# Which row groups a score group takes: chosen when it is issued, with longer planned GpSimd pieces and new seeds

## The chip, the cores and the metric

The kernel runs on one core of a Trainium2 chip. The metric is the time of one execution on the device in microseconds (us). Before the change three runs gave 784.35, 784.41 and 786.95 us; the median is 784.41 us. The core has five instruction queues that run beside each other: TensorE (PE, matmuls; its weight loads are listed as PEld), VectorE (DVE), ScalarE (ACT), GpSimd (POOL) and SyncE (SP, which issues the DMA transfers).

## What is computed

One transformer block with a conditioning vector, on 2048 tokens of width 512. Attention has 32 heads of width 16, so the 2048 x 2048 scores of 32 heads are the bulk of the element-wise work.

```python
mod = silu(c) @ w_mod                       # six vectors: sa, ca, ga, sb, cb, gb
h = layernorm(x) * (1 + ca) + sa
qkv = h @ wqkv                              # 32 heads of width 16
p = softmax(q @ k.T * 16 ** -0.5)           # per head, 2048 x 2048
x = x + ga * ((p @ v) @ wo)
h = layernorm(x) * (1 + cb) + sb
x = x + gb * (gelu(h @ w1 + b1) @ w2 + b2)  # inner width 1376
```

## The kernel before

**The score work.** Queries come in four blocks of 512, keys in sixteen tiles of 128 (`kt`). The work is cut into 32 runs (`runs`, `NR`, line 789), and a run handles four row groups at once: TensorE is used as four strips of 32 rows (`rows`, line 841), so that four matmuls with 32 rows each can run side by side, one for each strip. A run and a key tile give a tile of four score units, one for each row group; a unit is 128 keys x 512 queries. There are 32 x 16 x 4 = 2048 units.

**Two ways to exponentiate.** A unit goes one of two ways.

- ScalarE takes groups that alternate between three units and two (`SPAN`, line 306). `qk_a` (line 853) issues the matmuls of a group into a PSUM buffer `st` (there is one of each size), and one ScalarE instruction turns the group into `pt` (line 891). The three or two units follow each other through the tiles in the fixed order of row groups 0, 1, 2, 3: a tile's first three units may end one group, and its last one open the next (`at["A"]`, lines 802 and 856 to 864).
- VectorE takes whole tiles. `qk_d` (line 904) issues one matmul at a time into one of the two PSUM buffers `ax`, on any row group that the tile still lacks (the one that is free first, line 206), and VectorE writes the unit as a 16-bit integer into `ph` (line 933), which read as bf16 is a coarse power of two. Four shifted copies of the tile refine it (`shifts`, line 943): each is one VectorE instruction into `sh` (line 954), or, for the last of the four, four GpSimd pieces of one row group each into `sg` (`by_pool`, lines 962 to 975). The five versions are summed by TensorE, with V scaled in five ways (`VX`).

Of a run's sixteen tiles the five in `DKS` (line 302) may go to either engine: `next_tile` (line 821) gives them to VectorE, and ScalarE takes those that are left when its own are used up. So the share of each engine falls out of the order.

**Products, projections, tails.** `pv_op` (line 977) multiplies a tile by V into `od`, four matmuls side by side, accumulated over a run. `normalise` (line 1027) divides by the sums. When a block of queries is done, `block_tail` (line 1207) runs the output projection, the second layer norm (statistics and `z` on VectorE, `rs` on GpSimd, lines 622 to 638), its transposes, the two MLP matmuls, GELU on ScalarE, and the store. The last block is split in halves; `last_half` (line 1278) is what follows the last score.

**What sets the order.** The kernel writes its instruction order itself. `Plan` (line 107) keeps a clock for each engine, with planned durations given to each operation (`Op`), and again and again commits the operation that can start first (`step`, `pick`, `commit`). It is a list planner that runs when the program is built; the chip only sees the resulting queues. Parts of it that the change touches or that the text speaks of:

- `start` (line 135) gives the planned start of an operation. A score matmul group needs its row groups free (`pe_start`, `tiles`); an operation with `port` on VectorE or GpSimd waits until the other engine's planned piece with `port` is over.
- TensorE has three modes: scores (`qk`), products (`pv`) and the full array (`full`); a change costs 0.107 us in the plan (line 130).
- `G_US` (line 308) is the planned length of a GpSimd piece of `by_pool`, 0.65 us. A piece is planned beside a VectorE instruction that leaves room for it (`beside`, line 187).
- `heat` (line 447) puts filler matmuls with zeros where TensorE would otherwise be idle.
- Among operations that can start at about the same time, the one with the smallest priority value wins, to which `spread` (line 159) adds up to 0.15. That amount is a hash of the operation's kind (on TensorE) or of the source line of its function (other engines) with one of 32 numbers in `SEEDS` (line 64), one for each 25 us of planned time. Other seeds, or other line numbers, give another order.

Of the kernel before, what the change touches and what calls it, by code (L numbers as in the profile page):

```python
# [4 lines left out]

# [6 lines left out]
ACT = mybir.ActivationFunctionType  # L12
# [42 lines left out]
PEA = 0.38  # L55
# [4 lines left out]
DPL = 0.08  # L60
AL = 0.055
FILL = 2.1
SPREAD = 0.15
SEEDS = (925, 529, 257, 846, 939, 899, 560, 662, 544, 155, 536, 522, 19, 893, 450, 795, 742, 2, 4, 794, 818, 153, 176, 144, 484, 633, 742, 123, 569, 63, 333, 698)
HEAT = 1.7


class Res:


    def __init__(self, name, n, alloc):
        self.name, self.alloc = name, alloc
        self.free = [0.0] * n


class Op:
    count = 0

    def __init__(self, eng, fn, us, deps=(), lat=0.14, prio=5.0, mode=None, kind="", acq=None,
                 rel=(), gate=None, port=False):  # L80
        self.port = port
        self.eng, self.fn, self.us, self.lat, self.prio = eng, fn, us, lat, prio
        self.mode, self.kind, self.acq, self.rel, self.gate = mode, kind, acq, rel, gate
        self.end = None
        self.ready = 0.0
        self.tile = None
        self.slot = None
        self.kb, self.due, self.extra = 0, 1e9, False
        self.uses, self.use, self.alt = 0, 1.0, False
        self.rows, self.cont, self.run = None, False, None  # L90
        self.waiters = []
        self.todo = 0
        self.seq = Op.count
        Op.count += 1
        for d in deps:
            if d is None:
                continue
            if d.end is None:
                d.waiters.append(self)
                self.todo += 1  # L100
            else:
                self.ready = max(self.ready, d.end)
        for owner in rel:
            owner.uses += 1


class Plan:
    SLACK = {"NIL": 0.0, "PE": 0.10, "DVE": 0.05, "ACT": 0.15, "POOL": 0.05, "SP": 0.05}

    def __init__(self, dyn, later):  # L110
# [6 lines left out]
        self.dve = (0.0, 0.0, True)  # L117
        self.dyn, self.done, self.fill = dyn, deque(), FILL

# [13 lines left out]
        return max([self.free["PE"]] + [self.tiles.get(i, 0.0) for i in op.mode[1:]])  # L133

    def start(self, op):
        s = max(op.ready, self.pe_start(op) if op.eng == "PE" else self.free[op.eng])
        if op.acq is not None:
            s = max(s, min(op.acq.free))
        if op.eng == "PE" and self.later(op):
            s = max(s, self.fill_at)  # L140
        if op.port and op.us > 0:
            s = max(s, self.port["POOL" if op.eng == "DVE" else "DVE"])
        if op.kind == "beside":
            s = max(s, self.dve[0])
        return s

    def pick(self, eng):
# [11 lines left out]
    def spread(self, o):  # L159
        x = ((sum(map(ord, o.kind)) if o.eng == "PE" else o.fn.__code__.co_firstlineno if o.fn else 0) * 2654435761 ^ SEEDS[min(int(self.now // 25.0), len(SEEDS) - 1)] * 2246822519) & 0xFFFFFFFF  # L160
        x = ((x ^ x >> 15) * 2246822519) & 0xFFFFFFFF
        return SPREAD * ((x ^ x >> 13) & 1023) / 1024.0

# [106 lines left out]
def kernel(  # L270
# [14 lines left out]
    nc = tc.nc  # L285
    P = 128
    S = 2048
    D = 512
# [3 lines left out]
    QB = 512  # L292
# [12 lines left out]
    MM = 0.2155  # L305
    SPAN = (3, 2)
    POOL_US, POOL_MIN = 0.68, 0.5
    G_US, G_MIN, G_PRIO, G_MAX, G_FROM, G_TILES = 0.65, 0.5, 1.0, 4, 60.0, 6
    A_US = {1: 0.49, 2: 0.9165, 3: 1.3435}
    AHEAD = 3  # L310
    FIRST_DKS, D_TIME = (14,), 8.0
# [10 lines left out]
    def res(name, n, shape, dt, pool=work):  # L322
        return Res(name, n, lambda i: pool.tile(shape, dt, name=f"{name}{i}"))
# [3 lines left out]
    r_st = [res(f"st{n}", 1, [P, n * QB], FP32, ps) for n in SPAN]  # L327
    r_od = res("od", 1, [P, QB], FP32, pp)
    r_ax = res("ax", 2, [P, QB], FP32, pp)
    r_pt = [res(f"pt{n}_", NPT, [P, n * QB], BF16) for n in SPAN]  # L330
# [23 lines left out]
    units = [0]  # L354
    queued = deque()
# [45 lines left out]
    plan = Plan(dyn, later)  # L401
# [3 lines left out]
    def op(eng, *a, **k):  # L405
        o = Op(eng, *a, **k)
        if eng == "PE":
            o.due = due_now[0]
            due_now[0] += due_now[1]
        return plan.add(o)  # L410
# [108 lines left out]
    for h in range(2):  # L519
        o_x0 += 2 * [dma(lambda o, h=h: nc.sync.dma_start(out=o_x[0].tile[:, 2 * h:2 * h + 2, :],  # L520
                                                         in_=x_src[0][:, 2 * h:2 * h + 2, :]),
# [55 lines left out]
    for b in range(NQ):  # L577
        late = (lambda: True) if b == 0 else (lambda: first_ln[0])
# [9 lines left out]
    def silu(o):  # L588
# [8 lines left out]
              prio=0.0, rel=(o_tr,))  # L597
# [196 lines left out]
    def run_heads(r):  # L794
        b, u = runs[r]
        return (u % NC, None, u // NC) if b == LAST else (u // 2, u % 2, None)
# [2 lines left out]

    shared = [[kt for kt in (DKS if r else FIRST_DKS)] for r in range(NR)]  # L800
    own = [[kt for kt in range(NT) if kt not in shared[r]] for r in range(NR)]
    at = {"A": [0, 0, 3], "D": [0, 0, []]}
    turn = [0]

    o_e = {}
    left = [0] * NR
    begun = [False] * NR
    o_od = [None] * NR
# [2 lines left out]
    a_run = [0]  # L811
    pv_left = {}

    def d_run():
        for r in range(max(at["D"][0], a_run[0]), NR):
            if shared[r] and (r > a_run[0] or D_TIME < sum(queued) + 1.75 * (
                    len(own[r]) + len(shared[r]) - 1)):
                return r
        return NR

    def next_tile(which, r):
        while r < NR:
            if which == "A" and own[r]:
                return r, own[r].pop(0)
            if which == "A" and shared[r]:
                left[r] -= NPH - 1
                return r, shared[r].pop()
            if which == "D" and shared[r] and r >= d_run():
                return r, shared[r].pop(0)
            r += 1  # L830
        return None

    def qk(o, k, r, kt, i):
        b = runs[r][0]
        cc, par, hb = run_heads(r)
        kb, ko = divmod(kt, TPB)
        qm = o_q[(cc, b)][0]
        q_left[(cc, b)] -= 1
        if q_left[(cc, b)] == 0:
            qm.uses -= 1  # L840
        rows = slice(32 * i, 32 * i + 32)
        nc.tensor.matmul(out=o.tile[:, k * QB:(k + 1) * QB],  # L842
                         lhsT=kT[cc][kb][rows, ko * P:(ko + 1) * P],
                         rhs=qm.tile[rows, par, :] if hb is None else
                         qm.tile[rows, :, hb * HB:(hb + 1) * HB], start=True, stop=True)

    def qk_deps(r, kt):
        want_q(r // 2 + 1 if r < LAST * 8 else r - LAST * 4 + 2)
        cc, par, hb = run_heads(r)
        qm, evs = o_q[(cc, runs[r][0])]  # L850
        return [evs[par or 0], o_k[(cc, kt // TPB)]], qm

    def qk_a():
        got = []
        while len(got) < SPAN[turn[0]]:
            r, kt, i = at["A"]
            if i == 3:
                n = next_tile("A", r)
                if n is None:
                    break  # L860
                r, kt = n
            i = (i + 1) % 4
            at["A"][:] = r, kt, i
            got.append((r, kt, i))
        if not got:
            return
        n = turn[0]
        turn[0] = (n + 1) % len(SPAN)
        live["A"] += 1
        deps, rel = [], []  # L870
        for r, kt, i in got:
            d, qm = qk_deps(r, kt)
            deps += d
            if qm not in rel:
                rel.append(qm)

        def go(o):
            n_a[0] += 1
            queued.append(A_US[len(got)])
            a_run[0] = got[-1][0]  # L880
            for k, u in enumerate(got):
                qk(o, k, *u)
            live["A"] -= 1
        o = op("PE", go, MM, deps, lat=PEA, mode=("qk",) + tuple(u[2] for u in got), kind="qkA", acq=r_st[n],
               rel=rel, gate=lambda: n_a[0] - n_a[1] < 2)

        def ex(e):
            n_a[1] += 1
            queued.popleft()
            units[0] += len(got)  # L890
            nc.scalar.activation(out=e.tile[:, 0:len(got) * QB], in_=o.tile[:, 0:len(got) * QB],  # L891
                                 func=ACT.Exp, scale=ESC)
        e = op("ACT", ex, A_US[len(got)], (o,), lat=AL, prio=1.0, acq=r_pt[n], rel=(o,))
        e.uses += len({u[:2] for u in got})
        for k, (r, kt, i) in enumerate(got):
            o_e[(r, kt, i)] = (e, k)
            if i == 3:
                src = [o_e.pop((r, kt, m)) for m in range(4)]
                es = list({id(x): x for x, _ in src}.values())
                pv_op(r, kt, 0, es, lambda src=src: [x.tile[:, m * QB:(m + 1) * QB] for x, m in src], es)  # L900
                for x in es:
                    x.uses -= 1

    def qk_d():
        r, kt, rows = at["D"]
# [465 lines left out]
    for b in range(NQ):  # L1371
        kind = f"in{b}"
# [40 lines left out]

    state = {"late": 0}
    qk_a()
    want_q(1)
    while True:
        if not live["A"]:
            qk_a()
# [5 lines left out]
        while ended:  # L1425
            r = ended.pop(0)
            if r < NR - 1:
                normalise(r)
            b, u = runs[r]
# [77 lines left out]
```

## Time and profile before

| | |
|---|---|
| median of three runs | 784.41 us |
| profiled execution | 785.1 us |
| its span, first to last instruction | 783.2 us |
| mean granted TensorE clock | 0.998 of full |
| ScalarE: exponentials (line 891) | 624 groups, 710.8 us busy |
| VectorE: evacuations (line 933) | 488, 321.9 us |
| VectorE: shifted copies (line 954) | 405, 284.4 us |
| GpSimd: pieces of shifted copies (line 969) | 332, 205.3 us |
| first exponential starts, last ends | 14.54 us, 760.34 us |

A row of the profile's groups reads: line, engine, operation, output <- input with partitions x elements and type, how many; then busy time and the mean of one in ns; then the engine's idle time just before them and what ended most of it. Instructions of an engine can overlap at their ends, so the mean times the count can exceed the busy time. A row of the timeline reads: start, length, engine, line, operation, output <- input, how many were merged; in brackets the idle time ahead of it and what ended that.

### The profile page before, as it was taken

The page shows a single profiled execution, that of the slowest core. Times are in us where ns is not written, and L with a number is a line of the kernel's source. Part 1 is how long each engine was busy: PE and PEld are TensorE (multiplying, and loading weights), DVE is VectorE, ACT ScalarE, POOL GpSimd, SP SyncE. Part 2 cuts the span into 40 slices and gives each one's busy share as a digit, 9 for nine tenths or more (in the row PEclk, how much of TensorE's full clock was granted, in tenths as well). Part 3 has the DMA queues.
Part 4 walks back from the last instruction along what each step waited for, and adds up shares of the span by engine and source line. Part 5 has one row for each costly group of instructions (what it writes and reads, how often), then busy time and mean ns, then how long its engine had stood idle before and what let it go on. Part 6 is the DMA issues. An engine that isn't in the chain of part 4 may idle for free. (4 is left out here: it accounts for less than half of the span.)

```text
span 783.2 us, 21425 instructions
## 1 busy us (share of the span) xinstructions
PE 746.6 (95%) x8547; PEld 270.9 (35%) x8547; DVE 715.4 (91%) x1229; ACT 752.0 (96%) x675; POOL 337.3 (43%) x639
## 2 busy tenths in 40 slices
PE   8999999999999999999999999999999999989998
PEld 3433333233322232232332222222234434434444
DVE  6787778989999999999999998999899999997984
ACT  4999999999999999999999998999999999999994
POOL 6533545444445445552345243444243354343331
PEclk9999999999999999999999999999999999999999
DMA  7143011100110002000101000000111010100100
GB/s 216 37 151 63 19 23 44 26 16 10 46 52 22 5 17 66 20 9 17 46 21 34 23 19 16 20 23 26 29 42 35 8 41 18 46 19 22 25 18 28
DMA packets 38550, 27.75 MB, mean 35 GB/s; under 512 B 17941, under 2 KB 33846, under 8 KB 38450
## 3 DMA queue, kind: packets, MB, share of 16 engines
q1 hardware_dynamic: 38442, 26.39, 12.5%
q8 instruction: 67, 1.10, 0.6%
q14 instruction: 33, 0.27, 0.1%
q10 hardware_dynamic: 8, 0.00, 0.0%
HBM read 20.77 MB, written 2.61 MB: 30 GB/s over the span
## 5 line engine op out<-in xcount | busy, mean ns | idle before, releaser
L891 ACT ACTIVATE pt<-st 128x1536 bf16<-128x1536 f32 x624 | 710.8, 1302 | 8.3 <-PE st L842 5.7
L933 DVE TENSOR_SCALAR ph<-ax 128x512 int16<-128x512 f32 x488 | 321.9, 679 | 25.0 <-PE ax L842 22.0
L969 POOL TENSOR_SCALAR sg<-ph 128x512 int16<-128x512 int16 x332 | 205.3, 627 | 306.1 <-DVE sh L954 201.1
L954 DVE TENSOR_SCALAR sh<-ph 128x2048 int16<-128x2048 int16 x405 | 284.4, 723 | 4.1 <-PE od L1004 2.9
L842 PE MATMUL st<-qm,kT 32*128 32x512 bf16 x1560 | 245.9, 383 | 13.0 <-ACT pt L891 9.6
L842 PE MATMUL ax<-qm,kT 32*128 32x512 bf16 x488 | 170.2, 379 | 3.9 <-DVE ph L933 2.5
L842 PEld LDWEIGHTS <-kT 32*128 32x128 bf16 x2048 | 76.3, 91 | 229.3 <-issue 219.7
L1004 PE MATMUL od<-sh,VX 128*32 128x512 bf16 (+1 forms) x2024 | 145.3, 342 | 5.9 <-DVE sh L954 5.2
L1004 PE MATMUL od<-pt,VEB 128*32 128x512 bf16 (+1 forms) x1948 | 140.4, 340 | 0.1
L1004 PEld LDWEIGHTS <-VX 128*32 128x32 bf16 x2448 | 61.0, 95 | 89.5 <-issue 77.4
L1004 PEld LDWEIGHTS <-VEB 128*32 128x32 bf16 x2560 | 61.4, 96 | 77.2 <-issue 63.6
L1004 PE MATMUL od<-ph,VEB 128*32 128x512 bf16 (+1 forms) x612 | 48.6, 340 | 1.2 <-DVE OD L1029 1.1
L1237 PE MATMUL ax<-blk,W 128*128 128x512 bf16 (+1 forms) x176 | 44.6, 355 | 1.6 <-DVE ph L933 0.9
L776 POOL TENSOR_SCALAR VX<-VEB 128x128 bf16<-128x128 bf16 x80 | 27.6, 346 | 39.6 <-DVE VEB L652 35.0
L1056 POOL TENSOR_TENSOR OT<-OD,RB 128x256 bf16<-128x256 f32 x38 | 28.5, 764 | 28.7 <-DVE sh L954 18.5
L721 PE MATMUL ax<-blk,w 128*128 128x512 bf16 x124 | 35.6, 381 | 1.5 <-DVE ph L933 0.9
L1177 PE MATMUL ax<-w,g 128*128 128x512 bf16 x128 | 34.8, 382 | 1.2 <-DVE ph L933 1.2
L1004 PE MATMUL od<-sg,VX 128*32 128x512 bf16 (+1 forms) x424 | 34.4, 338 | 0.4 <-POOL sg L969 0.3
L467 PE MATMUL od<-warm 128*32 128x512 bf16 x320 | 31.5, 388 | 0.0
L1242 DVE TENSOR_SCALAR g<-ax,b1c 128x512 bf16<-128x512 f32 (+1 forms) x44 | 29.2, 673 | 0.4 <-PE ax L1237 0.3
L1056 POOL TENSOR_TENSOR OS<-OD,RB 128x256 bf16<-128x256 f32 x24 | 17.1, 728 | 18.2 <-DVE sh L954 18.1
L626 DVE BATCH_NORM_STATS2 ln_s<-xb 128x6 f32<-128x512 bf16 x32 | 21.6, 676 | 1.3 <-DMA xb<-in_A_x_dram 1.2
(108 smaller groups left out, 410.6 us busy)
## 6 DMA issues: line engine op xcount, KB each, us to landing
RB<-rn SPq DMA_DIRECT2D x124, 64.0 KB
xb<-in_A_x_dram SPq DMA_DIRECT2D x7, 512.0 KB
out_dram<-o SPq DMA_DIRECT2D x16, 128.0 KB
qm<-qs SPq DMA_DIRECT2D x120, 16.0 KB
W<-in_B_w_dram SPq DMA_DIRECT2D x1, 1376.0 KB
w<-in_A_wqkv_dram SPq DMA_DIRECT2D x3, 384.0 KB
blk<-in_w_mod_dram SPq DMA_DIRECT2D x2, 512.0 KB
g<-in_w_mod_dram SPq DMA_DIRECT2D x2, 512.0 KB
```

Of the source, the lines that this page charges most:

```text
L467: nc.tensor.matmul(out=o_od[r].tile[32 * i:32 * i + 32, :], lhsT=warm[:, 0:32], rhs=warm[:, 0:1].to_broadcast([P, QB]), start=False, stop= ...
L721: return chain([(lambda ps, j=j: nc.tensor.matmul(out=ps[:, 0:QB], lhsT=w.tile[:, j, cc * P:(cc + 1) * P], rhs=o_h[b].tile[:, j, :], start ...
L842: nc.tensor.matmul(out=o.tile[:, k * QB:(k + 1) * QB], lhsT=kT[cc][kb][rows, ko * P:(ko + 1) * P], rhs=qm.tile[rows, par, :] if hb is None ...
L891: nc.scalar.activation(out=e.tile[:, 0:len(got) * QB], in_=o.tile[:, 0:len(got) * QB], func=ACT.Exp, scale=ESC)
L933: nc.vector.tensor_scalar(out=ph.tile[:, o.row * QB:(o.row + 1) * QB], in0=o.tile, scalar1=PH_B, scalar2=0.0, op0=ALU.add, op1=ALU.max)
L954: nc.vector.tensor_scalar(out=o.tile, in0=first.tile, scalar1=PH_SH[j], scalar2=None, op0=ALU.add)
L969: after_dve(nc.gpsimd.tensor_scalar(out=sh.tile[:, c], in0=first.tile[:, c], scalar1=1.0, scalar2=float(PH_SH[j]), op0=ALU.mult, op1=ALU.add))
L1004: nc.tensor.matmul(out=o_od[r].tile[32 * i:32 * i + 32, n * HB:n * HB + w], lhsT=v_tile(kt, ph)[:, c0:c0 + 32], rhs=got[i][:, at:at + w], ...
L1056: two = beside(lambda c: nc.gpsimd.tensor_tensor(out=OT.tile[:, c], in0=OD.tile[:, c], in1=o5.tile[:, c], op=ALU.mult), (OT,), (OD, o5), f ...
L1177: nc.tensor.matmul(out=ps, lhsT=g[:, f, col:col + P], rhs=rhs, start=(f == 0), stop=(f == NF - 1))
L1237: mm = chain([(lambda ps, f=f, j=j, f0=f0: nc.tensor.matmul(out=ps[:, (f - f0) * N:(f - f0 + 1) * N], lhsT=W1[:, j, f * P:(f + 1) * P], rh ...
L1242: ev.append(op("DVE", lambda o, f=f, f0=f0, mm=mm: nc.vector.tensor_scalar(out=g.tile[:, f, 0:N], in0=mm.tile[:, (f - f0) * N:(f - f0 + 1) ...
```

## The change

- A ScalarE group no longer takes row groups in the fixed order. It is created with a number of units from one or two tiles (class `Tile` keeps which row groups a tile still lacks); which ones is chosen by `choose`, called each time its start is computed. `choose` tries the combinations and prefers the one whose row groups are free first; among equals, one that leaves a row group that VectorE's current tile still lacks. The tile's product with V then finds its four units by row group (`src`).
- `HOLD` is a longest time for which a ScalarE score group may be held back for a VectorE unit when TensorE is in another mode; it is 0.0, so that the new loop in `start` moves nothing.
- `G_US`, the planned length of a GpSimd piece, goes from 0.65 to 0.70 us.
- `SEEDS` has 32 other numbers. As lines are added, all later source lines move by 10 to 32, and these are part of the same hash.

No tile, buffer, data type or engine of an operation is changed.

```diff
@@ -1,5 +1,5 @@
 from collections import deque
-from itertools import islice
+from itertools import combinations, islice
 from contextlib import ExitStack
 import math
 
@@ -60,8 +60,9 @@
 DPL = 0.08
 AL = 0.055
 FILL = 2.1
+HOLD = 0.0
 SPREAD = 0.15
-SEEDS = (925, 529, 257, 846, 939, 899, 560, 662, 544, 155, 536, 522, 19, 893, 450, 795, 742, 2, 4, 794, 818, 153, 176, 144, 484, 633, 742, 123, 569, 63, 333, 698)
+SEEDS = (650, 213, 63, 336, 324, 364, 339, 395, 941, 438, 324, 33, 944, 780, 750, 866, 575, 626, 251, 357, 730, 442, 4, 383, 330, 53, 641, 829, 848, 541, 85, 264)
 HEAT = 1.7
 
 
@@ -86,6 +87,7 @@
         self.tile = None
         self.slot = None
         self.kb, self.due, self.extra = 0, 1e9, False
+        self.choose = None
         self.uses, self.use, self.alt = 0, 1.0, False
         self.rows, self.cont, self.run = None, False, None
         self.waiters = []
@@ -133,6 +135,8 @@
         return max([self.free["PE"]] + [self.tiles.get(i, 0.0) for i in op.mode[1:]])
 
     def start(self, op):
+        if op.choose is not None:
+            op.choose()
         s = max(op.ready, self.pe_start(op) if op.eng == "PE" else self.free[op.eng])
         if op.acq is not None:
             s = max(s, min(op.acq.free))
@@ -142,6 +146,12 @@
             s = max(s, self.port["POOL" if op.eng == "DVE" else "DVE"])
         if op.kind == "beside":
             s = max(s, self.dve[0])
+        if op.kind == "qkA" and self.mode != "qk":
+            for d in self.lists["PE"]:
+                if d.kind == "qkD" and d.gate():
+                    t = max(d.ready, min(d.acq.free))
+                    if s < t <= min(s + HOLD, self.need() - op.us - PEA - 0.02):
+                        s = t
         return s
 
     def pick(self, eng):
@@ -305,7 +315,7 @@
     MM = 0.2155
     SPAN = (3, 2)
     POOL_US, POOL_MIN = 0.68, 0.5
-    G_US, G_MIN, G_PRIO, G_MAX, G_FROM, G_TILES = 0.65, 0.5, 1.0, 4, 60.0, 6
+    G_US, G_MIN, G_PRIO, G_MAX, G_FROM, G_TILES = 0.70, 0.5, 1.0, 4, 60.0, 6
     A_US = {1: 0.49, 2: 0.9165, 3: 1.3435}
     AHEAD = 3
     FIRST_DKS, D_TIME = (14,), 8.0
@@ -799,10 +809,9 @@
 
     shared = [[kt for kt in (DKS if r else FIRST_DKS)] for r in range(NR)]
     own = [[kt for kt in range(NT) if kt not in shared[r]] for r in range(NR)]
-    at = {"A": [0, 0, 3], "D": [0, 0, []]}
+    at = {"A": [None, 0], "D": [0, 0, []]}
     turn = [0]
 
-    o_e = {}
     left = [0] * NR
     begun = [False] * NR
     o_od = [None] * NR
@@ -850,56 +859,79 @@
         qm, evs = o_q[(cc, runs[r][0])]
         return [evs[par or 0], o_k[(cc, kt // TPB)]], qm
 
+    class Tile:
+        def __init__(self, r, kt):
+            self.r, self.kt, self.rows, self.src, self.es = r, kt, [0, 1, 2, 3], {}, []
+
     def qk_a():
-        got = []
-        while len(got) < SPAN[turn[0]]:
-            r, kt, i = at["A"]
-            if i == 3:
-                n = next_tile("A", r)
-                if n is None:
+        got, want = [], SPAN[turn[0]]
+        while want:
+            cur, n = at["A"]
+            if n == 0:
+                nxt = next_tile("A", cur.r if cur else 0)
+                if nxt is None:
                     break
-                r, kt = n
-            i = (i + 1) % 4
-            at["A"][:] = r, kt, i
-            got.append((r, kt, i))
+                cur, n = Tile(*nxt), 4
+            c = min(n, want)
+            want -= c
+            at["A"][:] = cur, n - c
+            got.append((cur, c, c == n))
         if not got:
             return
         n = turn[0]
         turn[0] = (n + 1) % len(SPAN)
         live["A"] += 1
         deps, rel = [], []
-        for r, kt, i in got:
-            d, qm = qk_deps(r, kt)
+        for x, _, _ in got:
+            d, qm = qk_deps(x.r, x.kt)
             deps += d
             if qm not in rel:
                 rel.append(qm)
+        total = sum(c for _, c, _ in got)
+
+        def choose():
+            ks = got[0][1]
+            best = None
+            for head in combinations(got[0][0].rows, ks):
+                for tail in combinations([i for i in range(4) if i not in head], got[1][1] if len(got) > 1 else 0):
+                    busy = head + tail
+                    late = max(plan.tiles.get(i, 0.0) for i in busy) if plan.mode == "qk" else 0.0
+                    k = (max(late, plan.now), not any(i not in busy for i in at["D"][2] or range(4)))
+                    if best is None or k < best[0]:
+                        best = k, busy
+            o.mode = ("qk",) + best[1]
 
         def go(o):
             n_a[0] += 1
-            queued.append(A_US[len(got)])
-            a_run[0] = got[-1][0]
-            for k, u in enumerate(got):
-                qk(o, k, *u)
+            queued.append(A_US[total])
+            a_run[0] = got[-1][0].r
+            k = 0
+            for x, c, _ in got:
+                for i in o.mode[1 + k:1 + k + c]:
+                    qk(o, k, x.r, x.kt, i)
+                    x.rows.remove(i)
+                    x.src[i] = (e, k)
+                    k += 1
             live["A"] -= 1
-        o = op("PE", go, MM, deps, lat=PEA, mode=("qk",) + tuple(u[2] for u in got), kind="qkA", acq=r_st[n],
+        o = op("PE", go, MM, deps, lat=PEA, mode=("qk",) + tuple(range(total)), kind="qkA", acq=r_st[n],
                rel=rel, gate=lambda: n_a[0] - n_a[1] < 2)
+        o.choose = choose
 
         def ex(e):
             n_a[1] += 1
             queued.popleft()
-            units[0] += len(got)
-            nc.scalar.activation(out=e.tile[:, 0:len(got) * QB], in_=o.tile[:, 0:len(got) * QB],
+            units[0] += total
+            nc.scalar.activation(out=e.tile[:, 0:total * QB], in_=o.tile[:, 0:total * QB],
                                  func=ACT.Exp, scale=ESC)
-        e = op("ACT", ex, A_US[len(got)], (o,), lat=AL, prio=1.0, acq=r_pt[n], rel=(o,))
-        e.uses += len({u[:2] for u in got})
-        for k, (r, kt, i) in enumerate(got):
-            o_e[(r, kt, i)] = (e, k)
-            if i == 3:
-                src = [o_e.pop((r, kt, m)) for m in range(4)]
-                es = list({id(x): x for x, _ in src}.values())
-                pv_op(r, kt, 0, es, lambda src=src: [x.tile[:, m * QB:(m + 1) * QB] for x, m in src], es)
-                for x in es:
-                    x.uses -= 1
+        e = op("ACT", ex, A_US[total], (o,), lat=AL, prio=1.0, acq=r_pt[n], rel=(o,))
+        e.uses += len(got)
+        for x, _, full in got:
+            x.es.append(e)
+            if full:
+                pv_op(x.r, x.kt, 0, x.es, lambda x=x: [y.tile[:, m * QB:(m + 1) * QB] for y, m in (
+                    x.src[i] for i in range(4))], x.es)
+                for y in x.es:
+                    y.uses -= 1
 
     def qk_d():
         r, kt, rows = at["D"]
```

## The prediction

> **What bounds the kernel now.** First the busy times, then the costliest groups, both on the page.
>
> ```profile
> PE 746.6 (95%) x8547; PEld 270.9 (35%) x8547; DVE 715.4 (91%) x1229; ACT 752.0 (96%) x675; POOL 337.3 (43%) x639
> ...
> L891 ACT ACTIVATE pt<-st 128x1536 bf16<-128x1536 f32 x624 | 710.8, 1302 | 8.3 <-PE st L842 5.7
> L933 DVE TENSOR_SCALAR ph<-ax 128x512 int16<-128x512 f32 x488 | 321.9, 679 | 25.0 <-PE ax L842 22.0
> L969 POOL TENSOR_SCALAR sg<-ph 128x512 int16<-128x512 int16 x332 | 205.3, 627 | 306.1 <-DVE sh L954 201.1
> L954 DVE TENSOR_SCALAR sh<-ph 128x2048 int16<-128x2048 int16 x405 | 284.4, 723 | 4.1 <-PE od L1004 2.9
> ```
>
> Four engines share one job: 2048 score units of 128 x 512. ScalarE exponentiates 1560 of them (L891, groups of three and two units); VectorE makes the other 488 by integer arithmetic (L933, then four shifted copies of each tile of four units, at L954, or in four pieces on GpSimd, L969). ScalarE's 710.8 us hold only 8.3 us of waiting, so it is the pacemaker. Next I read busy time by stretches of 25 us (columns: stretch, length, then PE, weight loads, DVE, ACT, POOL, clock, DMA).
>
> ```profile
> 50.00:75.00 25.00, 24.90 (x243) 8.44 (x240) 21.04 (x40) 25.00 (x23) 5.03 (x15) 1.00 0.45 126
> 75.00:100.00 25.00, 24.10 (x263) 9.13 (x260) 19.08 (x31) 25.00 (x23) 16.01 (x32) 1.00 0.07 15
> 100.00:125.00 25.00, 23.88 (x253) 9.18 (x249) 20.54 (x34) 25.00 (x23) 12.01 (x22) 1.00 0.16 41
> 125.00:150.00 25.00, 24.52 (x281) 7.59 (x278) 22.81 (x43) 25.00 (x23) 11.56 (x18) 1.00 0.07 18
> ...
> 225.00:250.00 25.00, 23.74 (x253) 7.30 (x250) 25.00 (x43) 25.00 (x23) 12.76 (x21) 1.00 0.10 21
> ...
> 475.00:500.00 25.00, 24.19 (x248) 7.61 (x241) 23.92 (x41) 23.79 (x22) 9.58 (x15) 0.97 0.08 24
> ```
>
> Before 150 us VectorE has room, after 175 us nearly none (25.00 of 25 in one stretch). Between 25 and 750 us ScalarE is idle for 7.2 us in all: the gaps are what a better order can still win. The largest stands in the timeline near 473 us.
>
> ```profile
> 470.99 0.73 DVE L637 TENSOR_SCALAR z<-xb,mv,rs 128x512 bf16<-128x512 bf16 x2 [0.90 <-POOL rs L633]
> ...
> 472.38 0.38 PE L699 MATMUL ax<-ident,z 128*128 128x128 bf16 x4 [1.51 <-DVE ph L933]
> ...
> 473.30 1.45 ACT L891 ACTIVATE pt<-st 128x1536 bf16<-128x1536 f32 x1 [0.81 <-PE st L842]
> ...
> 476.21 2.44 ACT L891 ACTIVATE pt<-st 128x1024 bf16<-128x1024 f32 x2 [1.46 <-PE st L842]
> ```
>
> VectorE's z waited for GpSimd's rs; an evacuation behind z held a buffer of TensorE's transposes; TensorE stood 1.51 us with ScalarE's next scores queued behind. Then the clock fell: in five-us stretches it is 0.79 (470 to 475) and 0.87 (475 to 480), that is (0.21 + 0.13) x 5 / 0.5 = 3.4 us at half rate. ScalarE lost 0.81 + 1.46 = 2.27 us, the largest part of the 7.2.
>
> **The change part by part.** It changes no shape; it changes which unit goes to which engine, and the order. I compared the instruction lists of both programs.
>
> *ScalarE.* L891 has 624 groups now and 623 after: 311 of three, 311 of two, one of a single unit; 1556 units, four fewer. A pair (three and two) costs 710.8 / 312 = 2.278 us; 311 pairs cost 708.5. The group of one is in no row: pro rata 0.46 us (710.8 / 1560), from above 0.63 (ScalarE's cast of 128x512, 627 ns). I take 0.6, as the fixed cost of an instruction stays: 709.1, so -1.7 us (-1.8 to -1.6), straight on the pacing engine.
>
> *VectorE and GpSimd.* One key tile more on VectorE: 492 evacuations instead of 488; shifted copies 411 instead of 405, four for the tile and two taken back from GpSimd, whose pieces fall from 332 to 324 (two tiles of four). VectorE pays 4 x 0.660 (321.9 / 488) + 6 x 0.702 (284.4 / 405) = 6.85 us. What hides it: by the 97th ScalarE group the new order has ten more VectorE steps issued (177 against 167), and ten more is also the total at the end (1196 against 1186). That group runs at about 130 us (the 18th starts at 39.6 us, and 79 groups of 1.13 us lead from it to the 97th); in 50 to 150 us VectorE is idle for 3.96 + 5.92 + 4.46 + 2.19 = 16.5 us. So 0. Without that cover it is +6.85 (third rival).
>
> *TensorE.* Four more products with V, at 0.22 us each (two such sets start at 483.99 and 484.21 us): 0.9 us. Changes between score, product and full-array matmuls: 1305 before, 1328 after. One costs 0.10 us: from a product to the next scores it is 0.31 to 0.32 us start to start (484.21 to 484.53) where two products take 0.22. That is 2.3 us, 3.2 with the products. TensorE also has 20 more filler steps (63 to 83), issued only where nothing else can start, 20 x 0.22 = 4.4 us. I read these as room that covers the 3.2 us: 0 (0 to +3.2).
>
> The Trainium skill, TensorEngine Tiling (Array Packing), Key Properties, says that changing the tiling mode drains TensorE, which speaks against an order with more changes. The trace agrees, with 0.10 us each; were none of the 23 covered, the sum would be 2.3 us higher, 783.9 us.
>
> *The row choice itself.* A ScalarE group takes three or two of four row groups; a VectorE unit beside it can run at once only in another. Neighbouring pairs on a common row: ScalarE's first 51 before, 44 after; VectorE's first 42 and 45. Counting for each run of scores how often its most used row is passed, the sum is 729 before and 731 after, for the same 2048 units. The freedom gains nothing countable: 0, at most 4 pairs x 0.2 us = -0.8.
>
> *Longer GpSimd pieces* (0.65 to 0.70 us planned, 627 ns measured) and *new seeds* redraw the order everywhere; the source lines moved too, and they enter the same tie-break. Their price is that of the gaps: from -7.2 us (all gone) up to +4.5 (two more falls of the clock like that of 473 us). I take -1.1: the one known fall is an accident of one order, and I count half of its 2.27 us as gone, since the new lists have the same rs, z and transposes with GpSimd pieces ahead of rs at most of the seven places in the middle.
>
> *The tail.* Now the last exponential ends at 760.34 us, two GpSimd pieces run until 761.60, and the last product starts behind them.
>
> ```profile
> 754.80 5.54 ACT L891 ACTIVATE pt<-st 128x1024 bf16<-128x1024 f32 x5 [0.19 <-PE st L842]
> ...
> 760.39 1.20 POOL L969 TENSOR_SCALAR sg<-ph 128x512 int16<-128x512 int16 x2 [4.00 <-DVE g L1242]
> ...
> 761.64 0.38 PE L1004 MATMUL od<-sg,VX 128*32 128x256 bf16 x5 [0.30 <-POOL sg L969]
> ```
>
> Afterwards the last product hangs on a VectorE copy (0.68 us) behind two evacuations (0.87): no GpSimd piece, but 1.55 us in its place. I take 0, between -1.2 (the pieces' time gone) and +0.7. The rest of the tail has the same instructions. No DMA is added: 469 instructions on SP in both.
>
> *Sum:* -1.7 - 1.1 = -2.8 on the profiled execution's 785.1 us (span 783.2 and 1.9 around it): 782.3. The median of the runs is 0.7 below it (784.41), so **781.6 us**. Own range: 779 to 784.4.
>
> **Rivals.** (1) *The gaps thin out.* Without the fall of the clock and with half of the other 4.9 us, it is 784.4 - 1.7 - 2.3 - 2.5 = 777.9; 775.5 with no gap left. For it: most gaps (0.2 to 0.8 us) are a copy stretched beside GpSimd, with TensorE's next scores behind it, and longer planned pieces aim at these. Against it: those stretches come from all GpSimd work, not only these pieces.
>
> (2) *The change does not do what it says:* rows gain nothing, gaps return elsewhere, TensorE pays part of its 3.2 us: 784.4 - 1.7 + (1.7 to 4.8) = 784.4 to 787.5. For it: 731 against 729.
>
> (3) *Slower: VectorE becomes the bound.* Place: 175 to 700 us, where it is 98% busy. If the early lead is lost there (a z that waits for rs, as at 471 us), each lost us is paid, up to all 6.85 us: 784.4 + 6.85 - 1.7 = 789.6, and 791.3 if ScalarE's saving turns into waiting. It decides once over 5.6 us (3.9 + 1.7) of VectorE work lands on the path. Against it: the ten steps are done by 130 us, and the lead in scores holds later (461 against 456 at group 577).
>
> **Chances.** Forecast 0.45, (1) 0.25, (2) 0.17, (3) 0.13. About 0.5%, 3.9 us, is what a measurement can tell from no change: faster is below 780.5, slower above 788.3. The forecast's case gives 0.15 to faster; with (1) that is 0.40. Slower 0.13, within 0.47. The range leaves out the best half of (1) and all of (3) with the end of (2): 776.5 to 787.5.
>
> **What would show it.** L891 with 623 groups and about 709 us busy; idle before it near 6 us (forecast), under 4 (1), over 10 (2). The mean clock without a fall, or a fall with a stall of over 1 us ahead of it. VectorE about 7 us busier between 50 and 150 us; if it is so only after 175 us, my cover was wrong. The last exponential ends near 757.5 us, and 22.5 to 23 us follow it. The forecast is wrong if ScalarE's idle time moves by more than 3 us either way: its price is the one I could not read from a row.

## The result, and the profile after

The changed kernel takes 780.17 us (median of seven runs, 779.59 to 782.67) against 785.81 us for the kernel before beside it: a ratio of 0.9938, with a 95% interval of 0.9922 to 0.9954, or 4.9 us less (3.6 to 6.1; the ratio goes by the means, the two medians lie 5.6 us apart). A second measurement (e9 below) gave 0.9927 (0.9912 to 0.9943). The prediction was 781.6 us, faster, with a range of 776.5 to 787.5.

The busy times and the costliest groups of the page after (line 924 was 891, 965 was 933, 1001 was 969, 986 was 954):

```profile
PE 746.1 (96%) x8617; PEld 272.7 (35%) x8617; DVE 715.4 (92%) x1239; ACT 748.8 (96%) x674; POOL 331.1 (43%) x631
...
L924 ACT ACTIVATE pt<-st 128x1536 bf16<-128x1536 f32 x623 | 707.7, 1308 | 5.1 <-PE ax L851 2.0
L965 DVE TENSOR_SCALAR ph<-ax 128x512 int16<-128x512 f32 x492 | 323.5, 682 | 24.1 <-PE ax L851 21.3
L1001 POOL TENSOR_SCALAR sg<-ph 128x512 int16<-128x512 int16 x324 | 198.4, 621 | 285.6 <-DVE sh L986 211.7
L986 DVE TENSOR_SCALAR sh<-ph 128x2048 int16<-128x2048 int16 x411 | 278.1, 704 | 1.8 <-PE od L1036 0.9
```

ScalarE's exponentials are busy for 3.1 us less (710.8 to 707.7) and wait 3.2 us less (8.3 to 5.1). VectorE has ten instructions more in these two groups and the same busy time in all, 715.4 us: the copies' mean fell from 723 to 704 ns.

The profiled execution's span is 777.8 us, 5.4 less than before. It is the fastest of the seven, and its clock did not fall in the middle of the run as it does in the profile before; three of the other six had a mean clock of 0.995 or 0.996. Cut at the first and the last exponential it falls into three:

| stretch of the profiled execution | before | after |
|---|---|---|
| up to the first exponential | 14.5 us | 15.1 us |
| first to last exponential | 745.8 us | 739.5 us |
| of it, ScalarE idle | 8.8 us | 5.7 us |
| after the last exponential | 22.9 us | 23.2 us |

So all of the gain lies between the first and the last exponential. The start is no part of it: in other executions of the changed kernel's order the first exponential came at 13.95 and 14.53 us.

Busy time by stretches, after (columns as before; the third number behind the comma is VectorE):

```profile
50.00:75.00 25.00, 24.47 (x253) 8.74 (x252) 21.48 (x41) 25.00 (x24) 6.76 (x18) 1.00 0.44 126
75.00:100.00 25.00, 24.10 (x263) 10.34 (x259) 20.98 (x36) 24.82 (x23) 13.67 (x28) 1.00 0.06 16
100.00:125.00 25.00, 24.04 (x266) 8.23 (x258) 22.39 (x37) 25.00 (x24) 12.01 (x25) 1.00 0.13 36
125.00:150.00 25.00, 24.92 (x282) 7.97 (x278) 23.03 (x44) 24.99 (x24) 13.92 (x22) 1.00 0.09 24
150.00:175.00 25.00, 24.15 (x278) 8.60 (x270) 24.05 (x40) 25.00 (x24) 12.87 (x26) 1.00 0.05 14
```

The fifth stretch before:

```profile
150.00:175.00 25.00, 23.85 (x271) 7.99 (x269) 22.70 (x39) 24.93 (x23) 11.95 (x24) 1.00 0.08 21
```

VectorE's four stretches from 50 to 150 us sum to 87.9 us, against 83.5 before, and the fifth to 24.05 against 22.70. So VectorE did 5.8 us more work where it had been idle, and ScalarE stayed at 24.8 to 25.0 of 25 there.

The end of the score work, in the timeline after:

```profile
737.25 17.33 ACT L924 ACTIVATE pt<-st 128x1024 bf16<-128x1024 f32 x16 [0.26 <-PE st L851]
...
752.42 1.78 POOL L1001 TENSOR_SCALAR sg<-ph 128x512 int16<-128x512 int16 x3 [3.37 <-DVE g L1274]
...
755.52 0.69 DVE L986 TENSOR_SCALAR sh<-ph 128x2048 int16<-128x2048 int16 x1
...
756.25 0.40 PE L1036 MATMUL od<-sh,VX 128*32 128x256 bf16 x8
```

The last exponential ends at 754.58 us. The GpSimd pieces are done by 754.2, and the last product starts at 756.25, behind a copy on VectorE: 1.67 us after the exponential. Before, it was the product behind the GpSimd pieces that came last; its last five matmuls started 1.30 us after the exponential. One lag took the place of the other.

### The profile page after: what moved, and what is told of

Its sections match the earlier page's. It is cut to its first block, busy times and chain, and to the rows that moved or that the text cites. A ratio compares the mean times of both kernels' runs of the same rounds, so it can differ in the third digit from the quotient of the medians.

```text
span 777.8 us, 21575 instructions
## 1 busy us (share of the span) xinstructions
PE 746.1 (96%) x8617; PEld 272.7 (35%) x8617; DVE 715.4 (92%) x1239; ACT 748.8 (96%) x674; POOL 331.1 (43%) x631
## 4 chain that ended last, share of the span: by engine, by line
PE 46%; ACT 27%; DVE 16%; issue 7%; DMA 2%; POOL 1%; SPq 0%; DVEq 0%; POOLq 0%; ACTq 0%
ACT pt L924 25%; PE od L1036 15%; PE st L851 13%; DVE ph L965 6%; DVE sh L986 5%; PE ax L1209 5%; PE ax L851 3%; PE ax L1269 3%; PE ax L731 2%; DMA dc<-dn 2%; PE od L477 1%; PE ax L1203 1%; DVE xb L1252 1%; PE ax L461 1%; PE ax L770 1%
## 5 line engine op out<-in xcount | busy, mean ns | idle before, releaser
L924 ACT ACTIVATE pt<-st 128x1536 bf16<-128x1536 f32 x623 | 707.7, 1308 | 5.1 <-PE ax L851 2.0
L1001 POOL TENSOR_SCALAR sg<-ph 128x512 int16<-128x512 int16 x324 | 198.4, 621 | 285.6 <-DVE sh L986 211.7
L986 DVE TENSOR_SCALAR sh<-ph 128x2048 int16<-128x2048 int16 x411 | 278.1, 704 | 1.8 <-PE od L1036 0.9
L851 PE MATMUL ax<-qm,kT 32*128 32x512 bf16 x492 | 166.4, 379 | 2.0 <-DVE ph L965 1.2
L1036 PE MATMUL od<-sh,VX 128*32 128x512 bf16 (+1 forms) x2048 | 147.3, 342 | 5.3 <-DVE sh L986 4.2
L477 PE MATMUL od<-warm 128*32 128x512 bf16 x368 | 34.8, 382 | 0.0
L1036 PE MATMUL od<-sg,VX 128*32 128x512 bf16 (+1 forms) x416 | 32.8, 337 | 0.6 <-POOL sg L1001 0.5
```

Of the source, the lines that this page charges most:

```text
L477: nc.tensor.matmul(out=o_od[r].tile[32 * i:32 * i + 32, :], lhsT=warm[:, 0:32], rhs=warm[:, 0:1].to_broadcast([P, QB]), start=False, stop= ...
L851: nc.tensor.matmul(out=o.tile[:, k * QB:(k + 1) * QB], lhsT=kT[cc][kb][rows, ko * P:(ko + 1) * P], rhs=qm.tile[rows, par, :] if hb is None ...
L924: nc.scalar.activation(out=e.tile[:, 0:total * QB], in_=o.tile[:, 0:total * QB], func=ACT.Exp, scale=ESC)
L986: nc.vector.tensor_scalar(out=o.tile, in0=first.tile, scalar1=PH_SH[j], scalar2=None, op0=ALU.add)
L1001: after_dve(nc.gpsimd.tensor_scalar(out=sh.tile[:, c], in0=first.tile[:, c], scalar1=1.0, scalar2=float(PH_SH[j]), op0=ALU.mult, op1=ALU.add))
L1036: nc.tensor.matmul(out=o_od[r].tile[32 * i:32 * i + 32, n * HB:n * HB + w], lhsT=v_tile(kt, ph)[:, c0:c0 + 32], rhs=got[i][:, at:at + w], ...
```

## The experiments

Line numbers enter the planner's tie-break, so every variant keeps each line where it was. A variant that edits the plan has another order throughout; one that edits only which row groups are written out keeps the order of every instruction.

**e1: old seeds.** Only the seeds go back.

```diff
-SEEDS = (650, 213, 63, 336, 324, 364, 339, 395, 941, 438, 324, 33, 944, 780, 750, 866, 575, 626, 251, 357, 730, 442, 4, 383, 330, 53, 641, 829, 848, 541, 85, 264)
+SEEDS = (925, 529, 257, 846, 939, 899, 560, 662, 544, 155, 536, 522, 19, 893, 450, 795, 742, 2, 4, 794, 818, 153, 176, 144, 484, 633, 742, 123, 569, 63, 333, 698)
```

> The changed kernel with the 32 seeds of before; row choice and 0.70 us pieces stay. Its instruction list has 1564 units on ScalarE (626 groups) against 1556. Theory (the gain is that of one good order, found by its seeds: fewer ScalarE units and fewer gaps): 8 units x 0.455 us = +3.6 us, and the gaps between 25 and 750 us back to some 7 us from 4.7, so about 786 us, nothing left of the gain. Rival A (the row choice earns the gain): at most 782 us. Rival B (the longer planned pieces earn it): at most 782 us as well.

Measured: 793.94 us, ratio 1.0117 (1.0099 to 1.0136), slower than the kernel before. The theory's sign held (nothing was left of the gain) and its number, 786 us, failed: from the first to the last exponential it took 744.5 us, less than before the change, but 32.0 us followed the last one. The timeline there:

```profile
762.45 1.58 PE L1269 MATMUL ax<-blk,W 128*128 128x256 bf16 x13
...
764.67 1.28 ACT L1279 ACT_TABLE_LOAD   x1 [5.01 <-DVE g L1274]
```

ScalarE had run out of scores and waited 5.01 us for the last block's MLP, whose matmuls (line 1269) TensorE only then came to. 56 steps of that block's tail stood behind the last scores in TensorE's queue; in the changed kernel it is 7.

**e2: GpSimd pieces planned at 0.65 us again.**

```diff
-    G_US, G_MIN, G_PRIO, G_MAX, G_FROM, G_TILES = 0.70, 0.5, 1.0, 4, 60.0, 6
+    G_US, G_MIN, G_PRIO, G_MAX, G_FROM, G_TILES = 0.65, 0.5, 1.0, 4, 60.0, 6
```

> The changed kernel with GpSimd pieces planned at 0.65 us as before; row choice and new seeds stay. 1560 units on ScalarE, 340 GpSimd pieces. Theory (one good order; any edit redraws it): +1.8 us for four units and gaps of 6 to 9 us, 783 to 787 us. Rival A (row choice): about 780 us, 782 at most. Rival B (pieces): back to 785 us or more, with more VectorE copies stretched (mean of a copy near 723 ns against 704).

Measured: 790.65 us, ratio 1.0068 (1.0056 to 1.0080). Rival A fell, and the theory's 787 us were too few: ScalarE is idle for 10.7 us between first and last exponential, and 27.3 us follow the last. The mean of a copy went back to 719 ns and the time to over 785 us, as rival B says; whether the copies are the cause, or the other order, this run alone can't tell. The next one shows whether the longer pieces are enough by themselves.

**e3: fixed row groups.** The plan again takes them in turn.

```diff
-            o.mode = ("qk",) + best[1]
+            o.mode = ("qk",) + tuple(got[0][0].rows[:ks]) + tuple(range(got[1][1] if len(got) > 1 else 0))
```

> The changed kernel with the row groups of a ScalarE group in the fixed order of before; 0.70 us pieces and new seeds stay. 1560 units. Theory (one good order): 783 to 787 us like the other two. Rival A (row choice): back to 785 us, and clearly slower than the run with 0.65 us pieces. Rival B: about 780 us.

Measured: 790.39 us, ratio 1.0056 (1.0042 to 1.0070). With the longer pieces kept the loss is nearly that of e2, so rival B fell as well: neither edit carries the gain by itself. The number is beyond the theory's 787, too (idle 12.6 us).

**e4: the kernel before with the new seeds** (the same line of seeds, the other way round).

> The kernel before with the 32 new seeds only. 1560 units as before, 324 GpSimd pieces. Theory (seeds fit only the program they were picked for): no gain, 784 to 790 us with gaps of 7 us or more. Rival C (the new seeds are better in themselves): 782 us or less. Rivals A and B: 785 to 786 us.

Measured: 795.87 us, ratio 1.0135 (1.0119 to 1.0152). Rival C fell: the new numbers are not better in themselves.

**e5 and e10: the same order, rows put back.** Only the row group that each ScalarE matmul uses is changed as it is written out; all five instruction lists keep their order.

```diff
-            self.r, self.kt, self.rows, self.src, self.es = r, kt, [0, 1, 2, 3], {}, []
+            self.r, self.kt, self.rows, self.src, self.es, self.todo = r, kt, [0, 1, 2, 3], {}, [], [0, 1, 2, 3]
...
                 for i in o.mode[1 + k:1 + k + c]:
+                    x.rows.remove(i); i = x.todo.pop(0)
                     qk(o, k, x.r, x.kt, i)
-                    x.rows.remove(i)
                     x.src[i] = (e, k)
```

> The changed kernel in exactly its order of instructions; only the row groups that a ScalarE group's matmuls use are put back to 0, 1, 2, 3 in turn when they are written out (80 of 623 groups differ). In this order the most used row is passed 761 times instead of 731, so TensorE has 30 passes more. The step on record (the choice gains nothing, at most 0.8 us): 780 to 781 us. Rival A (the choice earns the gain, its passes lie on ScalarE's path): 30 x 0.22 = 6.6 us, up to 786.8 us, ScalarE's gaps some 6 us longer. Between them (part lies in TensorE's holes): 782 to 785 us.

Measured: 781.21 us, ratio 0.9955 (0.9941 to 0.9969), 1.0 us over the changed kernel's first median. That is small, and the two were measured at different times, so it was repeated beside the changed kernel (e9):

> The changed kernel as it is, beside the next three on one chip. All theories: 780 us (779.6 to 782.7 in the runs so far, the longer ones with a clock of 0.995 or 0.996).

> The same order with the row groups put back to 0, 1, 2, 3 in turn, a second time, for the difference to the changed kernel on one chip. If the choice of rows saves what the first run showed: +0.7 to +1.5 us over the changed kernel, some 0.04 us for each of the 30 passes. If that was chance: within 0.4 us of it. Rival A (nearly all of the gain): +4 us or more.

Measured: e9 779.09 us, ratio 0.9927 (0.9912 to 0.9943); e10 781.87 us, ratio 0.9961 (0.9947 to 0.9975). The row choice is worth 2.8 us here, more than the 1.5 expected, and the intervals do not overlap. It is not a matter of the clock alone: among the executions with a mean clock of 0.999 or 1.0, e9 took 778.1 to 779.0 us and e10 781.1 to 781.6, 2.4 us between the medians (in the first comparison 779.9 and 781.4). The exponentials of both, by shape, e9 first:

```profile
L924 ACT ACTIVATE pt<-st 128x1536 bf16<-128x1536 f32 x311 | 473.8, 1523 | 2.2 <-PE st L851 1.0 <-PE ax L851 0.6 <-PE od L1036 0.2
L924 ACT ACTIVATE pt<-st 128x1024 bf16<-128x1024 f32 x311 | 342.0, 1100 | 2.8 <-PE ax L851 1.4 <-PE od L1036 0.9 <-PE st L851 0.4
```

```profile
L924 ACT ACTIVATE pt<-st 128x1536 bf16<-128x1536 f32 x311 | 470.4, 1513 | 3.8 <-PE ax L851 1.8 <-PE st L851 1.0 <-PE od L1036 0.2
L924 ACT ACTIVATE pt<-st 128x1024 bf16<-128x1024 f32 x311 | 338.7, 1089 | 2.6 <-PE od L1036 0.9 <-PE ax L851 0.8 <-PE st L851 0.7
```

Idle time grows from 5.0 to 6.4 us, most of it in the groups of three, where the part that ended with scores into VectorE's buffer `ax` goes from 0.6 to 1.8 us (in the groups of two it falls from 1.4 to 0.8). That fits a ScalarE group that waits in TensorE's queue for a row group that a VectorE unit is using; no run shows that wait by itself. The busy time of the same 622 groups grows as well, though each is shorter: they overlap less. One place in e9 and then in e10, from ScalarE's timeline:

```profile
573.30 17.08 ACT L924 ACTIVATE pt<-st 128x1024 bf16<-128x1024 f32 x15
```

```profile
573.72 4.69 ACT L924 ACTIVATE pt<-st 128x1536 bf16<-128x1536 f32 x4
578.66 11.60 ACT L924 ACTIVATE pt<-st 128x1536 bf16<-128x1536 f32 x10 [0.25 <-PE ax L851]
```

In e10 ScalarE stands idle for 0.25 us, until scores into `ax` are done; in e9 that stretch has no gap.

The largest difference is elsewhere, and the row groups are not its only cause. ScalarE's timeline near 196 us, e9 and then e10:

```profile
194.74 1.02 ACT L924 ACTIVATE pt<-st 128x1024 bf16<-128x1024 f32 x1 [0.76 <-PE ax L851]
196.07 135.39 ACT L924 ACTIVATE pt<-st 128x1536 bf16<-128x1536 f32 x119 [0.31 <-PE ax L851]
```

```profile
195.36 1.02 ACT L924 ACTIVATE pt<-st 128x1024 bf16<-128x1024 f32 x1 [0.58 <-PE ax L851]
197.17 2.37 ACT L924 ACTIVATE pt<-st 128x1536 bf16<-128x1536 f32 x2 [0.78 <-PE ax L851]
200.08 133.07 ACT L924 ACTIVATE pt<-st 128x1536 bf16<-128x1536 f32 x117 [0.55 <-PE ax L851]
```

Here ScalarE loses 1.07 us in one and 1.91 in the other. But the clock fell there in e10, and not in e9 (third number from the end, e9 first):

```profile
195.00:200.00 5.00, 4.88 (x55) 1.40 (x56) 5.00 (x9) 4.66 (x5) 2.08 (x4) 1.00 0.19 57
```

```profile
195.00:200.00 5.00, 5.00 (x44) 1.21 (x41) 4.68 (x8) 3.39 (x3) 1.76 (x3) 0.66 0.20 59
```

That is (1 - 0.66) x 5 / 0.5 = 3.4 us at half rate. From the first to the last exponential e10 takes 2.9 us more than e9: compared exponential by exponential, that is 0.8 us of idle time at this fall, 0.6 us of idle time elsewhere, and 1.4 us of lost overlap, elsewhere too. The profiles of e5 and of the changed kernel differ in the same way (2.7 us, 0.9 of it at a fall at the same place that e5 alone has). Whether the row groups bring on the fall is not shown; it is not in every execution of e10 (three of six have a mean clock of 0.999 or 1.0). Over the whole, ScalarE is idle 5.5 against 7.0 us between first and last exponential; what follows the last is 23.3 us in both.

**e6: old seeds from the 25th on.** The order is the same up to 600 us of planned time.

```diff
-SEEDS = (650, 213, 63, 336, 324, 364, 339, 395, 941, 438, 324, 33, 944, 780, 750, 866, 575, 626, 251, 357, 730, 442, 4, 383, 330, 53, 641, 829, 848, 541, 85, 264)
+SEEDS = (650, 213, 63, 336, 324, 364, 339, 395, 941, 438, 324, 33, 944, 780, 750, 866, 575, 626, 251, 357, 730, 442, 4, 383, 484, 633, 742, 123, 569, 63, 333, 698)
```

> The changed kernel with the old seeds from the 25th on, so its order is the same up to 600 us of planned time and drawn anew after that; 1556 units as before the edit. Theory (an order is good in its gaps and in how far VectorE lags when the last exponential ends): gaps before 600 us as in the changed kernel (4.4 us), and a longer stretch after the last exponential than 23.2 us: 782 to 790 us in all. Rival (only the count of ScalarE units and the early gaps matter): 780 to 781 us.

Measured: 783.56 us, ratio 0.9991 (0.9980 to 1.0003). As the theory says: idle 6.4 us, and 25.8 us after the last exponential, with 15 products left behind the last scores instead of 7. A new draw of the last quarter alone takes back most of the gain.

**e7 and e8: random seeds**, the same 32 in both kernels.

```diff
+SEEDS = (137, 582, 867, 821, 782, 64, 261, 120, 507, 779, 460, 483, 667, 388, 807, 214, 96, 499, 29, 914, 855, 399, 443, 622, 780, 785, 2, 712, 456, 272, 738, 821)
```

> The changed kernel with 32 random seeds; 1568 units on ScalarE. Theory (an undirected draw is worse than a picked one): 786 to 796 us: +5.5 us for twelve units more, gaps of 7 to 12 us, and what follows the last exponential between 23 and 32 us. Rival A (the row choice carries it whatever the seeds): at most 784 us.

> The kernel before with the same 32 random seeds; 1568 units. Theory: 788 to 798 us, of the same kind as the changed kernel with these seeds, a few us more since its row groups are fixed. Rival (picked seeds do not matter): 784 to 786 us.

Measured, one execution each: 790.24 and 785.17 us. The second is a miss: undirected seeds serve the kernel before as well as its own (784.95 us). It has eight units more on ScalarE, and makes up for them with 5.1 us of idle time instead of 8.8 and nothing left over at the end. So a random draw need not give a bad order, and the row choice does not carry a bad one: with these seeds the changed kernel is the slower of the two.

**e11 and e12: best rows for a known order.** As in e5, but each tile's order of row groups is read from a table worked out once the order is known, so that a run of scores passes its most used row as seldom as it can.

```diff
-            self.r, self.kt, self.rows, self.src, self.es, self.todo = r, kt, [0, 1, 2, 3], {}, [], [0, 1, 2, 3]
+            self.r, self.kt, self.rows, self.src, self.es, self.todo = r, kt, [0, 1, 2, 3], {}, [], next_rows()
```

The kernel before, which names its units in advance, gets the same kind of table `tn`:

```diff
-                qk(o, k, *u)
+                qk(o, k, u[0], u[1], int(tn[u[:2]][u[2]]))
...
-                src = [o_e.pop((r, kt, m)) for m in range(4)]
+                src = [o_e.pop((r, kt, tn[(r, kt)].index(str(m)))) for m in range(4)]
```

> The changed kernel's order once more, but the row groups of all ScalarE groups picked after the order is known, so that a run of scores passes its most used row as seldom as can be: 675 passes instead of 731. If a pass is worth 0.04 us: -2.2 us, about 778 us, faster than both kernels. If the passes that are left lie in TensorE's holes: no change, 780 us. If every pass were on ScalarE's path (0.22 us): 768 us.

> The kernel before in exactly its order, with its row groups picked in the same way: 669 passes instead of 729. If a pass is worth 0.04 us in this order too: -2.4 us, about 782.4 us. If the choice of rows helps only with the new order: 784.7 us as before.

Measured: e11 778.99 us, ratio 0.9925 (0.9909 to 0.9942), the same as e9; e12 783.16 us, ratio 0.9980 (0.9971 to 0.9990), 1.8 us less than the kernel before. So row groups help in the old order too, but not by the pass: 30 passes are worth 1.0 to 2.8 us, the next 56 nothing that could be measured. The passes that are left seem to lie where ScalarE does not wait (it is idle for 5.2 us in e11, 5.5 in e9), which no run shows by itself. No variant is clearly faster than the changed kernel.

All orders side by side (stretches from the profiled executions; "steps left" are the TensorE steps of the last block's tail behind the last scores, from the instruction lists; the time before is the median of its 17 runs beside e9):

| kernel | time, us | units on ScalarE | first to last exponential | of it idle | after the last | steps left |
|---|---|---|---|---|---|---|
| before | 784.95 | 1560 | 745.8 | 8.8 | 22.9 | 0 |
| changed | 780.17 | 1556 | 739.5 | 5.7 | 23.2 | 7 |
| e1 | 793.94 | 1564 | 744.5 | 7.0 | 32.0 | 56 |
| e2 | 790.65 | 1560 | 747.8 | 10.7 | 27.3 | 44 |
| e3 | 790.39 | 1560 | 749.1 | 12.6 | 25.3 | 17 |
| e4 | 795.87 | 1560 | 747.9 | 11.7 | 30.0 | 45 |
| e7 | 790.24 | 1568 | 746.0 | 7.2 | 24.5 | 12 |
| e8 | 785.17 | 1568 | 744.6 | 5.1 | 22.8 | 0 |

In these eight the stretch after the last exponential grows with the steps left, from 22.8 us to 32.0; e7 also started 2 to 3.5 us later than the others. e6 is not in the table: its 25.8 us come with products left behind, not with such steps.

## Why the prediction was right, and what it mis-sized

*ScalarE's units, -1.7 us.* Right. With the rows put back (e10) the new order's exponentials are busy 709.0 us against 710.8: -1.8.

*The gaps, -1.1 us.* The right sign, by luck in part: in e10 the idle time between first and last exponential is 7.0 us against 8.8, so -1.8. The stall and the fall of the clock near 473 us, half of whose price I had counted as gone, are gone in the profile after. But in e10 the clock falls once all the same, at 196 us, and three of the changed kernel's seven runs had a mean clock of 0.995 or 0.996: the new order did not do away with such falls. By the prediction's own sign of being wrong, ScalarE's idle time moving by more than 3 us, it was just over the line (8.8 to 5.7 us); the part beyond -1.8 came from the row choice and from the fall that the profile after lacks.

*VectorE's cover, 0.* The cover was there: VectorE was 4.4 us busier from 50 to 150 us (about 7 were forecast) and 5.8 by 175, with 0.2 us of gaps on ScalarE, and for this order the rival in which VectorE becomes the bound fell. Whether the cover alone would have done is not shown, as VectorE's copies got shorter by more than the tile costs (below). One reading was off: from 175 to 700 us VectorE had been busy for 509.8 of 525 us, 97% and not 98%.

*The row choice itself, 0, at most -0.8 us.* This is the term that was mis-sized: it measured -2.8 us beside the changed kernel (e9 and e10) and -1.0 in the first comparison. The count behind it set the passes of the old order, 729, against those of the new one, 731. These are two different orders; in one and the same order, fixed rows pass 761 times and chosen ones 731. And the price is not that of a pass: of 2.9 us between the profiles of e9 and e10, half is idle time, 0.8 us of it where the clock fell in e10, and half is exponentials that overlap less (707.5 against 709.0 us busy for the same 623 groups), a loss that no idle column shows. With the rows put back the new order takes 781.9 us (e10), where the forecast, with nothing for this term, had 781.6; the chosen rows do the rest.

*TensorE's 23 changes of mode and four products, 0.* Not isolated. With the rows put back, all of the order's 3.1 us (785 x (1 - 0.9961)) is made up of -1.8 for units, -1.8 for gaps and +0.4 after the last exponential, which leaves nothing for them.

*The tail, 0 (-1.2 to +0.7).* +0.4 us, by the exchange of one lag for another.

*Longer pieces.* They have no effect on the chip but through the order. The mean of a VectorE copy was 723, 719, 717 and 713 ns in the four orders planned with 0.65 us (before, e2, e4, e8) and 702 to 710 in those planned with 0.70 (changed, e1, e3, e6, e7). For 411 copies, the 19 ns between before and changed are 7.8 us of VectorE, more than the added tile costs, and so its busy time did not grow. That is a regular difference over these orders (e6 shares most of its order with the changed kernel), not a test by itself: e2, which alone isolates the edit, moves the whole order too.

*Rival 1, thinner gaps,* came halfway: idle time fell by 3.1 us, not by 4.8. *Rival 2* had the row choice and the gaps wrong. The time lies 0.3 us beyond the line that the prediction drew for faster (780.5 us), to which it gave a chance of 0.40. What the prediction did not see is how far a redraw of the order can go: between 785 and 796 us for six undirected ones; in the slowest two, e1 and e4, the stretch after the last exponential is 7 to 9 us longer than before. That this draw of seeds was good was no finding of mine; only the range made room for it.

What stays open: how much of the order's 3.1 us a fair average over many seeds would leave to the longer pieces.

## What to carry to other kernels

Where a planner writes the order, compare an edit's direct effect in one and the same order: hold the order and change only what the edit hands to the chip. A gain that vanishes when an unrelated tie-break is redrawn is a property of that order, and has to be measured again after every edit, line shifts included. And read the pacing engine's busy time beside its idle time: work that arrives just in time costs overlap before it costs a gap.

## What the runs showed of the hardware

*Overlap of exponentials.* In the kernel before, 312 groups at 1513 ns and 312 at 1090 ns sum to 812.1 us, but are busy for 710.8: each overlaps its neighbour by 162 ns in the mean. In e9 it is 175 ns (311 x 2.623 + 0.6 = 816.4 us against 707.5), in e10, the same order with the rows put back, 162 ns again (809.8 us against 709.0): half of the difference between these two profiles lies there. The Trainium skill, ScalarE: Activation LUTs, What ACT_TABLE_LOAD costs, gives about 93 ns for this overlap; in these traces it is larger, and it depends on how early the next group's scores stand ready. In e9 it is 77 ns in the mean where the last score matmul of a group ends (by the profile's modelled ends) 150 to 200 ns before the exponential ahead, 136 ns at 250 to 300, and 178 to 211 ns from 300 on.

*The clock falls in some executions of the same program.* The kernel before ran 42 times beside the experiments: 3 runs at a mean clock of 1.0 took 783.0, 783.5 and 783.7 us, those at 0.998 had medians of 784.7 to 785.1, those at 0.996 or less took 785.7 to 786.9. One fall of 3.4 us at half rate is 0.002 of the span, so a fall costs about 1.5 us (an estimate from these groups of runs; at the one fall in e10 it was 0.8 us). The Trainium skill, TensorE: Matmul & The Clock Gate, What's actually happening, says that the gate halves the rate after at least one idle window of some 3.4 us, and that these windows run freely, whatever the kernel does. The length of the fall agrees, and so does its coming in some runs only; the idle time does not: before the fall at 473 us TensorE had stood still for 1.51 us. Windows show in the clock records: in each profile the time from one change of the clock to the next is a whole multiple of 3.413 us (467.63 us, 137 of them, up to the fall at 472.87). Near 192 us TensorE stands still in the profiles of the changed kernel, e5, e9 and e10. In e5 and e10 the 1.52 and 1.35 us lie within one window, and the clock falls at its end; in the changed kernel and e9 the 1.70 and 1.53 us lie across the border of two, and it does not. How much idle time in a window it takes is not shown: e2 and e7 have falls with no stand over 0.5 us in the window ahead.
